# A sliding-window attention and feed-forward kernel: a new order of the first phase, and Q of the last three batches transposed by the DMA crossbar

## The chip, the cores and the metric

The kernel runs on one core of a Trainium2 chip. The metric is the time of one execution in device microseconds (us); lower is better. The profiled execution also has a span, from its first to its last instruction, which is one or two microseconds below the time. PE is TensorE's matmul stream, PEld its weight loads, DVE is VectorE, ACT is ScalarE, POOL is GpSimd and SP is SyncE, which issues most of the DMAs.

## The reference

Eight batches of eight heads, 576 positions, head size 64. Each query sees itself and the 63 positions before it. The result of the attention, 4608 rows of 512, goes through a feed-forward part without a nonlinearity other than a product:

```python
scores = scale * np.matmul(q, k.transpose(0, 1, 3, 2))
rel = pos[:, None] - pos[None, :]
mask = (rel >= 0) & (rel < 64)
attn = softmax(np.where(mask, scores, -1e9))        # cut: written out in the reference
x = (attn @ v).transpose(0, 2, 1, 3).reshape(B * S, H * D)
a = x @ w1
b = x @ w2
h = a * b @ w3
return h @ w_out
```

## The kernel before

The kernel folds `w3 @ w_out` into one matrix `wc` in its first phase. From there it runs as one pipeline. A tick places half a step of attention among the matmuls of the feed-forward part (FFN), twelve ticks to a batch. Q and K come as float32 rows, are cast to float16, transposed by TensorE into PSUM and copied back:

```python
def big_rows(which, b, hh):
    return {"k": k, "q": q, "v": v}[which][b, hh:H:2].rearrange("j (p r) d -> p j (r d)", r=TI)   # p (32) is outermost

def load_qk(b, which, gate=None, other=None):
    t = sb.tile([P, 2, TI * D], FP32, name="stage", bufs=3)
    ...
    for hh in range(2):
        (other if hh and other else nc.sync).dma_start(out=t[:, hh], in_=big_rows(which, b, hh))

def load_v(b, *blocks):                 # GpSimd's queue: casts on the way, rows of 64
    vh = v_heads(b)
    for c in blocks:
        ...
        nc.gpsimd.dma_start(out=vh[lo:P, c], in_=v[b, :, s0:s0 + P - lo, :].rearrange("h s d -> s h d"))

def copy_v(b, c):                       # the overlap of two blocks of V, on VectorE
    vh = v_heads(b)
    dve_cp(vh[0:D, c], vh[D:P, c - 1])
    if c == 1:
        dve_cp(vh[D:P, 1], vh[0:D, 2])

def transposes(b, which, *cs, into=None, cps=None):
    ...
    for c, tp in zip(cs, into):
        for i in range(6):
            nc.tensor.transpose(tp[:, i, :], t16[:, 6 * c + i, :], ident16)
    # cut: the copies out of PSUM
```

The events of a batch stand in a table. The key is the tick; each event names how many batches ahead it works:

```python
late = {0: [("t", 1, "k", 0), ("cast", 1, "q", 0)], 1: [("cast", 1, "q", 1)],
        2: [("t", 1, "k", 1), ("load", 2, "k")], 4: [("t", 1, "k", 2), ("v", 1, 0, 2, 3)],
        5: [("load", 2, "q")], 6: [("t", 1, "q", 0), ("v", 1, 4, 5)], 7: [("cast", 2, "k", 0)],
        8: [("t", 1, "q", 1), ("copy", 1, 4)], 9: [("copy", 1, 1), ("cast", 2, "k", 1)], 10: [("t", 1, "q", 2)]}
```

The output leaves in blocks of 128 rows from three buffers named `t2k`, filled by VectorE and stored from SyncE's queue, the one that also loads K and Q:

```python
def store():
    while stores:
        r0, c0, c1, o_sb = stores.pop(0)
        queue = nc.scalar if c1 - c0 < DM and c0 == 0 else nc.sync
        queue.dma_start(out=out[r0:r0 + P, c0:c1], in_=o_sb[:, c0:c1])
```

## Time and profile before

| | before |
|---|---|
| time, median of 3 runs | 292.44 us (292.0 to 293.64) |
| span of the profiled execution | 291.4 us |
| TensorE busy | 275.1 us, 94% |
| next busiest: VectorE, GpSimd | 183.6 us, 180.0 us |
| V of batch 5, issue to landing | 2.6 to 4.5 us |

### The profile page before, as it was taken

What the parts mean: (1) busy time and instruction counts of PE and PEld (TensorE: products, weight loads), DVE (VectorE), ACT (ScalarE), POOL (GpSimd) and SP (SyncE); (2) the same over time, 40 slices, a digit from 0 to 9 for tenths busy, and PEclk for the clock granted to TensorE, in tenths of its full rate; (3) what the DMA queues carried; (4) which work ended last, traced back from release to release, by engine and by line L of the source; (5) the groups of instructions that cost most, each with busy time, mean ns of one, the idle gap of its engine ahead of it and who ended that gap; (6) DMA issues with size and microseconds to landing.
All of it is one profiled execution on the core that took longest, in us unless ns stands there. A gap on an engine that the chain in (4) does not pass through costs nothing.

```text
span 291.4 us, 6248 instructions
## 1 busy us (share of the span) xinstructions
PE 275.1 (94%) x2429; PEld 161.4 (55%) x2429; DVE 183.6 (63%) x280; ACT 167.9 (58%) x277; POOL 180.0 (62%) x215
## 2 busy tenths in 40 slices
PE   7589998989899999999999999999999999999992
PEld 7468885445554555555555787455555545444441
DVE  0946558635868477678687856587866655454531
ACT  2565644675267746866777556487567765642300
POOL 8779933599479938695789363786596444402200
PEclk9999999999999999999999999999999999999998
DMA  6999999919697848194849560940094011002013
GB/s 242 247 209 204 207 217 374 168 14 94 152 364 126 77 131 317 12 107 131 311 30 126 168 231 0 187 44 2 37 165 30 2 73 73 2 36 110 2 39 112
DMA packets 48449, 37.68 MB, mean 129 GB/s; under 512 B 34160, under 2 KB 38512, under 8 KB 48416
## 3 DMA queue, kind: packets, MB, share of 16 engines
q0 software_dynamic: 38960, 11.14, 37.1%
q1 hardware_dynamic: 9024, 24.79, 23.4%
q10 hardware_dynamic: 432, 1.31, 1.3%
q8 instruction: 20, 0.33, 0.4%
q14 instruction: 13, 0.11, 0.1%
HBM read 38.80 MB, written 9.44 MB: 166 GB/s over the span
## 4 chain that ended last, share of the span: by engine, by line
PE 80%; POOL 7%; DVE 6%; ACT 2%; DMA 2%; issue 1%; DVEq 0%; POOLq 0%; SPq 0%; ACTq 0%
PE f_ps L432 38%; PE f_ps L450 20%; PE o_ps L354 5%; PE tp L262 5%; PE f_ps L501 5%; PE s_ps L296 4%; POOL pt L310 2%; POOL pt L308 2%; DMA stage<-in_k_dram 2%; DVE kT L266 1%; POOL v L241 1%; DVE k L229 1%; ACT pt L300 1%; PE f_ps L492 1%; PE s_ps L338 1%
## 5 line engine op out<-in xcount | busy, mean ns | idle before, releaser
L432 PE MATMUL f_ps<-xT,w_sb 128*128 128x512 f16 (+1 forms) x640 | 134.4, 358 | 0.0
L308 POOL TENSOR_SCALAR_AFFINE_SELECT pt<-pt 128x512 f16<-128x512 f16 (+1 forms) x64 | 52.5, 820 | 62.3 <-ACT pt L300 62.3
L432 PEld LDWEIGHTS <-w_sb 128*128 128x128 f16 x640 | 59.7, 98 | 50.3 <-issue 0.3
L450 PE MATMUL f_ps<-wc_sb,ab 128*128 128x512 f16 (+1 forms) x296 | 67.0, 373 | 0.1
L438 DVE TENSOR_TENSOR ab<-f_ps,a_sb 128x512 f16<-128x512 f32 x72 | 49.8, 691 | 22.1 <-PE f_ps L432 18.6
L300 ACT ACTIVATE pt<-s_ps 128x1024 f16<-128x1024 f32 (+1 forms) x48 | 45.7, 952 | 21.5 <-PE s_ps L296 19.1
L437 ACT COPY a_sb<-f_ps 128x512 f32<-128x512 f32 x72 | 41.7, 580 | 27.8 <-PE f_ps L432 26.8
L310 POOL TENSOR_SCALAR_AFFINE_SELECT pt<-pt 128x512 f16<-128x512 f16 (+1 forms) x64 | 52.1, 814 | 4.5
L363 DVE TENSOR_TENSOR xT<-o_ps,r 64x384 f16<-64x384 f32 x36 | 19.8, 550 | 39.8 <-ACT r L362 39.8
L450 PEld LDWEIGHTS <-ab 128*128 128x128 f16 x296 | 27.5, 98 | 27.9 <-issue 0.3
L360 ACT ACTIVATE ln_s<-o_ps 64x384 f32<-64x384 f32 x36 | 17.5, 487 | 32.6 <-PE o_ps L354 32.6
L452 DVE COPY t2k<-f_ps 128x512 f32<-128x512 f32 (+1 forms) x36 | 24.5, 682 | 11.8 <-PE f_ps L450 11.4
L241 POOL DMA_DIRECT2D v<-in_v_dram x35 | 29.6, 861 | 0.0
L354 PEld LDWEIGHTS <-v 128*128 128x128 f16 x288 | 18.1, 98 | 8.7 <-ACT pt L300 0.8
L296 PEld LDWEIGHTS <-kT 64*128 64x128 f16 x384 | 10.9, 94 | 18.6 <-issue 16.8
L354 PE MATMUL o_ps<-pt,v 128*128 128x128 f16 (+1 forms) x288 | 20.7, 215 | 0.4 <-DVE xT L364 0.4
L226 POOL CAST k<-stage 128x1152 f16<-128x1152 f32 x12 | 13.7, 1150 | 11.0 <-PE s_ps L262 8.1
L364 DVE TENSOR_TENSOR xT<-o_ps,r 64x384 f16<-64x384 f32 x36 | 20.2, 561 | 0.5
L296 PE MATMUL s_ps<-qT,kT 64*128 64x128 f16 (+1 forms) x384 | 18.2, 214 | 1.8 <-ACT pt L300 1.4
L362 ACT ACTIVATE r<-ln_s 128x384 f32<-128x384 f32 x36 | 18.8, 523 | 1.1
L361 ACT ACTIVATE ln_s<-o_ps 64x384 f32<-64x384 f32 x36 | 17.4, 482 | 0.4
L266 DVE COPY kT<-tp 128x768 f16<-128x768 f16 x18 | 17.1, 950 | 0.0
(88 smaller groups left out, 236.5 us busy)
## 6 DMA issues: line engine op xcount, KB each, us to landing
out_dram<-t2k SPq DMA_DIRECT2D x35, 256.0 KB
stage<-in_k_dram SPq DMA_DIRECT2D x13, 576.0 KB
stage<-in_q_dram SPq DMA_DIRECT2D x13, 576.0 KB
v<-in_v_dram POOLq DMA_DIRECT2D x28, 128.0 KB, 4.3
w_sb<-in_moe_w_dram POOLq DMA_DIRECT2D x4, 512.0 KB, 11.1
ab<-in_moe_w_dram POOLq DMA_DIRECT2D x2, 512.0 KB, 10.7
ab<-in_moe_w_out_dram POOLq DMA_DIRECT2D x2, 512.0 KB, 14.5
xT<-in_moe_w_dram POOLq DMA_DIRECT2D x2, 512.0 KB, 16.3
```

Source lines behind the costliest of these rows:

```text
L241: nc.gpsimd.dma_start(out=vh[lo:P, c], in_=v[b, :, s0:s0 + P - lo, :].rearrange("h s d -> s h d"))
L296: nc.tensor.matmul(s_ps[:, a, jj, c0:c0 + n], kT[half, j, k0:k0 + P], qT[half, j, q0:q0 + n], start=True, stop=True, skip_group_check=True)
L300: nc.scalar.activation(pt[:, :, :, 0:w], s_ps[:, :, :, 0:w], AF.Exp, bias=-SHIFT, scale=scale)
L308: nc.gpsimd.affine_select(out=sl, in_=sl, pattern=pat, compare_op=ALU.is_ge, fill=0.0, base=off, channel_multiplier=-1)
L310: nc.gpsimd.affine_select(out=sl, in_=sl, pattern=[[-s, m] for s, m in pat], compare_op=ALU.is_ge, fill=0.0, base=63 - off, channel_multip ...
L354: nc.tensor.matmul(o_ps[:, jj, o0:o0 + n], v16[:, si * 2 + bi, j0 + jj, a * D:a * D + P], pt[:, a, jj, c0:c0 + n], start=first, stop=(bi = ...
L364: nc.vector.tensor_tensor(xs[D:P], o_ps[D:P, :, 192:384], r[D:P], ALU.mult)
L432: nc.tensor.matmul(d[:, f * n + c0:f * n + c1], w[:, dc, (fc + f) * P:(fc + f + 1) * P], xT[:, dc, xc:xc + c1 - c0], start=first, stop=(dc ...
L437: act_cp(a_sb[:, 0:nf * n], a_ps[:, 0:nf * n])
L438: nc.vector.tensor_tensor(ab[:, fc:fc + nf, lo:hi], b_ps[:, 0:nf * n].rearrange("p (f n) -> p f n", f=nf), a_sb[:, 0:nf * n].rearrange("p ...
L450: nc.tensor.matmul(o_ps[:, 0:c1 - c0], ab[:, fc, t * P:t * P + P], wc_sb[:, fc, c0:c1], start=(fc == 0), stop=(fc == 7))
L452: cp(o_sb[:, c0:c1], o_ps[:, 0:c1 - c0])
```

## The change

Part one reorders the first phase: casts and copies a little earlier, an FFN unit between each two steps that depend on each other, and the second buffer of V filled with ones earlier. Part two lets the DMA crossbar transpose Q of batches 5 to 7 (`CROSSED = 5`), so that TensorE and the copies out of PSUM are spared that work. One such transpose is called a crossing below. Positions 0 to 511 of each batch are crossed in one go; positions 512 to 575 are loaded together (`"last"`) and crossed together, and that for all eight batches. To let the crossbar write plain rows, the queries stay in a permuted order in the scores, and the exponential puts them back in order.

```diff
+    def crossed(b, which):
+        return which == "q" and (b == "last" or b >= CROSSED)
     ...
         for hh in range(2):
-            (other if hh and other else nc.sync).dma_start(out=t[:, hh], in_=big_rows(which, b, hh))
+            if not crossed(b, which):
+                (other if hh and other else nc.sync).dma_start(out=t[:, hh], in_=big_rows(which, b, hh))
+            elif b == "last":
+                src = q.rearrange("b (j e) s d -> e (b j) s d", e=2)[hh, :, TP * QI:S]
+                nc.sync.dma_start(out=t[:, hh, 0:QI * D], in_=src.rearrange("j (p r) d -> j p (r d)", r=QI))
+            else:
+                nc.sync.dma_start(out=t[:, hh, 0:QI * D],
+                                  in_=q[b, hh:H:2, 0:TP * QI].rearrange("j (p r) d -> j p (r d)", r=QI))
     ...
+    def turn(b):
+        t = ...                                             # cut: a tile of the pool "rows" or "vT"
+        tr = t.rearrange("p a n -> p (a n)")[:, 0:QI * P].rearrange("p (i n) -> p i n", i=QI)
+        nc.sync.dma_start_transpose(tr, t16s["q", b][:, 0:QI].rearrange("q i n -> q (i n)"))
+        turned["q", b] = tr
     ...
+                    nc.tensor.matmul(o[:, :, 0:mid - p0], kT[half, j, k0:k0 + P], qT[half, :, TP * j + p0:TP * j + mid], ...)
+                    if p1 > TP:                             # the queries past 512 lie in the other tile
+                        nc.tensor.matmul(o[:, :, mid - p0:p1 - p0], kT[half, j, k0:k0 + P], turned["q", "last"][...], ...)
     ...
-    late = {0: [("t", 1, "k", 0), ("cast", 1, "q", 0)], 1: [("cast", 1, "q", 1)],
-            2: [("t", 1, "k", 1), ("load", 2, "k")], 4: [("t", 1, "k", 2), ("v", 1, 0, 2, 3)],
+    late = {0: [("t", 1, "k", 0), ("cast", 1, "q", 0)],
+            1: [("cast", 1, "q", 1), ("turn", 1), ("load", "last", "q")],
+            2: [("t", 1, "k", 1), ("load", 2, "k")],
+            3: [("cast", "last", "q", 0, pool_cp), ("cast", "last", "q", 1, pool_cp), ("turn", "last")],
+            4: [("t", 1, "k", 2), ("v", 1, 0, 2, 3)],
     ... (the first phase; its part that matters below:)
     scores(6)
-    ffn_ab(0, 3)
-    scores(7)
     copy_v(1, 1)
     ...
+    ffn_ab(0, 3)
+    scores(7)
+    copy_v(1, 4)
     ffn_ab(0, 4)
     scores(8)
-    copy_v(1, 4)
```

## The prediction

> **What bounds the kernel now.** I read the stretches first: the busy time of each engine in nine windows of the span (columns: stretch, its length, then busy microseconds and instruction counts of PE, PEld, DVE, ACT and POOL, the granted clock, the DMA share, GB/s).
>
> ```profile
> 0.00:20.00 20.00, 14.30 (x195) 12.87 (x195) 9.26 (x9) 9.46 (x11) 15.89 (x23) 1.00 0.99 235
> 20.00:44.10 24.10, 22.89 (x327) 19.60 (x325) 14.51 (x24) 13.06 (x23) 18.77 (x24) 1.00 1.23 212
> 44.10:78.80 34.70, 31.24 (x314) 17.05 (x313) 21.70 (x32) 18.51 (x30) 23.39 (x27) 1.00 0.91 158
> ...
> 120.00:160.00 40.00, 40.00 (x336) 21.34 (x335) 30.35 (x46) 28.22 (x48) 33.49 (x38) 1.00 0.74 129
> 160.00:200.00 40.00, 40.00 (x367) 26.83 (x365) 28.45 (x45) 25.24 (x43) 23.73 (x29) 1.00 0.52 116
> 200.00:240.00 40.00, 40.00 (x319) 20.49 (x317) 26.99 (x44) 27.96 (x48) 25.53 (x33) 1.00 0.35 56
> ```
>
> From 120 to 240 us TensorE has no gap and no other engine is full. There every microsecond taken from TensorE is a microsecond of the end, and one taken from another engine is nothing. Gaps lie in the first 79 us: 5.7, 1.2 and 3.5 us in the first three stretches. I then read TensorE's timeline there for what ends each gap (columns: start, length, instruction, count, idle time before it and its releaser):
>
> ```profile
> 22.46 0.51 PE L262 MATMUL o_ps<-ident,k 128*128 128x128 f16 x6 [1.02 <-DVE k L226]
> ...
> 49.94 0.50 PE L262 MATMUL o_ps<-ident,q 128*128 128x128 f16 x6 [1.19 <-DVE q L226]
> 50.27 0.50 PE L262 MATMUL tp<-ident,q 128*128 128x128 f16 x6
> 50.61 0.50 PE L262 MATMUL s_ps<-ident,q 128*128 128x128 f16 x6
> ...
> 61.07 0.40 PE L296 MATMUL s_ps<-qT,kT 64*128 64x128 f16 x8 [1.06 <-ACT pt L300]
> ...
> 78.16 0.49 PE L262 MATMUL tp<-ident,q 128*128 128x128 f16 x6 [0.98 <-DVE kT L266]
> ```
>
> All four are matters of order: a cast or copy on VectorE placed too late (22.5 and 49.9), scores too close behind the previous ones for their only PSUM buffer (61.1), one transposition bank still being emptied (78.2). Third, the DMA of 39 to 59 us, in 40 slices of half a microsecond:
>
> ```profile
> DMA  9999999999999999999999999999999999980000
> GB/s 209 207 203 205 207 238 194 173 325 326 409 345 387 360 372 390 370 379 373 398 369 382 353 398 362 390 369 328 198 158 153 154 147 77 50 53 0 0 0 0
> ```
>
> SyncE's loads of K and Q (576 KB each) run at 330 to 400 GB/s until about 53 us; what follows to 57 us is V of batch 1. Its blocks, issued from 34.8 us, took 19.5 to 20.2 us to land (54.3 for the first, about 55.5 for the second); V of batch 2 took 2.6 to 4.6.
>
> [...]
> [...]above, six transpositions start every 0.34 us, 56 ns each.
> [...]
> [...]
> [...]
>
> **Part one, the order of the first phase.** Engine by engine, in the new program order with the old durations:
> - The memset of the second V buffer (2.7 us) moves ahead of GpSimd's weight loads. The first K and Q loads keep the DMA engines full to about 9 us (396 to 433 GB/s from 3.5 to 8.5), so a weight load issued at 6.7 instead of 4.0 finds its turn at about the same time. I count nothing.
> - Weight folding of blocks 2 and 3 now stands before V's transpositions, where four dummy matmuls (0.2) and the wait of 1.02 were. VectorE reaches the cast of V later, so part comes back: I estimate the phase's last fold ends near 42.4, not 44.1.
> - K and Q of batch 1 are cast before they are needed: the 1.19 us gap goes. Scores 6 then run at about 49.7 instead of 52.8, 3 us early.
> - Here a new wait takes it back. The copies between V blocks of batch 1 now follow scores 6 directly on VectorE, at about 50.4, and their data lands at about 55.5, because GpSimd's issue and SyncE's traffic do not move. VectorE stands in order behind them: copies 0.3 + 0.4, then the product of FFN block 3, 0.69, done near 56.9. TensorE has three FFN banks; it can finish block 4 and scores 8 (about 54.2), but block 5 needs the bank which that product frees. It starts near 56.9; before it started at 57.3. Of 3 us, 0.4 is left and TensorE idles about 2.7.
> - From there to the first FFN product of the next group TensorE has seven units of 1.73, three scores of 0.33, six values of 0.5 to 0.57 and six transposition groups of 0.34: 12.1 + 1.0 + 3.3 + 2.0 = 18.4 us. Before, this took 57.3 to 78.8, 21.5, the difference being the gaps of 1.06, 0.98 and 0.23 and smaller ones. The new order sets an FFN unit between each dependent pair, so I take 18.5: 75.4 instead of 78.8.
> GpSimd must keep pace: from scores 6 on it has 19.9 us of masking, casts and V issues, as before (54.1 to 74.0); begun near 51.1 it ends near 71, and the last values need it at 71.8. It just fits.
> Part one: **-3.4 us**.
>
> **Part two, Q of batches 5 to 7 through the crossbar.** These groups carry it (count, then busy us and mean ns):
>
> ```profile
> L262 PE MATMUL tp<-ident,q 128*128 128x128 f16 x108 | 9.1, 220 | 1.0 <-DVE kT L266 1.0
> L266 DVE COPY qT<-tp 128x768 f16<-128x768 f16 x11 | 10.4, 948 | 0.1
> L300 ACT ACTIVATE pt<-s_ps 128x768 f16<-128x768 f32 x16 | 13.0, 811 | 5.3 <-PE s_ps L296 4.9
> L226 POOL CAST q<-stage 128x1152 f16<-128x1152 f32 x12 | 13.4, 1147 | 0.1
> ```
>
> - TensorE loses 3 x 18 = 54 transpositions: 54 x 56 ns = 3.0 us, all in the gapless stretch.
> - It gains matmuls: queries past 512 lie in another tile, so in the last third of each batch one 128-column matmul of each head becomes two of 64: 8 heads x 3 batches = 24 more. In the timeline eight score matmuls of 128 columns take 0.33 us (41 ns each); four of 128 and four of 64 take 0.27, so a 64 costs 26 ns. A split costs 2 x 26 - 41 = 11 ns; 24 of them 0.26 us.
> - Strides: the moving operand is read in runs of eight halves (16 bytes)[...]; split outputs are runs of four floats.[...] I count 0, as the least certain term.
> - VectorE loses 6 copies (5.7 us), ScalarE 3 of 0.81. ScalarE's exponential of the first third is split in two (512 columns about 0.58, 256 about 0.37, by its copies of those sizes): 0.95 for 0.81, six times, +0.8. It reads PSUM with a step, but its strided copies of 768 elements take 809 ns, just what a plain 768 exponential takes, so the step is free. None of it is on the path.
> - GpSimd: six casts shorter by a ninth (-0.8), two more (+2.0). The new ones stand among the masks near 148 us, where GpSimd is 84% busy; they wait for their own load and the crossbar's read of the previous tile. Three ticks of 2.4 us lie between scores and values, so about 4 us of delay is absorbed.
> - DMA: four transposes of 512 KB.[...] The first is ready at about 142 (cast before: 139.9 to 142.2) and needed near 166: 23 us of slack.
> Part two: -3.0 + 0.26 = **-2.7 us**.
>
> Sum: -3.4 - 2.7 = -6.1, from 292.4 to 286.3. I add half a microsecond for small waits in a rearranged pipeline: **286.8**.
>
> **The rivals.**
> - V lands earlier, or VectorE is not held: then part one could reach 5.5 us and the end 284. For: 3 us lie ready at scores 6. Against: the DMA stays full to 57, and GpSimd's 19.9 us chain then binds about 2 us later.
> - Strided matmuls are slow. If the 18 score units of three batches took double (0.33 us more), 6 us come back and the time is 292.[...]
> - The crossbar takes over 20 us a transpose, or holds SyncE's queue. GpSimd's cast into the same tile then waits in order ahead of the masks, TensorE stops twice or more: 295 to 310. For: it is untested here, and K of batch 6 queues behind it.[...]
> - The early memset delays the first weights: at most 2.7 us at the start, 289.
>
> **Range and chances.** The two gains are nearly independent. With both halved the time is 289.5; with V early 284; the slow crossbar, one in twelve, lies outside. Range 283.0 to 291.5. The 2% line is 286.6, almost on my centre: faster 0.46, same 0.46, slower 0.08.
>
> **What would show each step.** Right: scores 6 near 50 us, then a TensorE gap of 2 to 3 us ahead of FFN block 5 that traces back to V's landing; the next group's first FFN product near 75.5; TensorE gapless from 120 on; 54 fewer transpositions and 24 more score matmuls; crossbar DMAs landing in single microseconds. Wrong: no such gap; score matmuls of batches 5 to 7 well above 0.33 us for eight; idle on TensorE near 150 to 190 released by GpSimd or a DMA.

Its sum came to -3.4 - 2.7 = -6.1 us, from 292.4 to 286.3, and to 286.8 with half a microsecond added for small waits.

## More of the kernel before

The page cuts the span in 40 slices of about 7.3 us; a digit is the busy share in tenths. Two of its rows are TensorE's busy share and the clock granted to it:

```profile
PE   7589998989899999999999999999999999999992
PEclk9999999999999999999999999999999999999998
```

After the first third no slice but the last is below nine tenths, and the clock falls only in the last. SyncE's timeline in the middle of the kernel (start, length of issue, what it issues, how many) becomes important later:

```profile
135.83 1.27 SPq L210 DMA_DIRECT2D stage<-in_k_dram  x2
...
137.88 1.19 SPq L210 DMA_DIRECT2D stage<-in_q_dram  x2
...
156.33 2.54 SPq L459 DMA_DIRECT2D out_dram<-t2k  x2
```

K and Q of batch 6 are asked for at 136 to 139 us, in a pause between two groups of output stores. Another view, of the instructions that touch V from 140 to 175 us, gives the times of its loads:

```profile
L241 POOL DMA_DIRECT2D v<-in_v_dram x5: 692/896/900, 149.1 to 154.7; - x5
...
DMA to landing us min/median/max: 2.6/3.6/4.5
```

V of batch 5 is issued from 149.1 us on, when the Q load of 137.9 is done, and lands within 4.5 us.

## The result, and the profile after

The changed kernel takes 312.85 us (median of 4 runs, 311.27 to 314.76) against 292.22 us for the kernel before in the same rounds: 7% slower. The ratio is 1.0703, with a 95% interval of 1.0625 to 1.0781. A ratio here and below is the mean time of one kernel's fast runs over that of the other's fast runs of the same rounds, so it is not quite the ratio of the medians quoted. The prediction, 286.8 with a range up to 291.5, was wrong.

The same two rows of the page, now with slices of 7.7 us:

```profile
PE   8699999699999999999870599949999999999994
PEclk9999999999999999999996599987999999999999
```

Slices 21 to 23 hold a hole, slice 27 another. The granted clock falls to 0.6 and 0.5 in slices 22 and 23, and to 0.8 and 0.7 around slice 28. The stretches say how much (columns: stretch, its length, busy us and instruction counts of PE, PEld, DVE, ACT, POOL, granted clock, DMA share, GB/s):

```profile
120.00:160.00 40.00, 38.17 (x306) 19.72 (x307) 25.35 (x39) 26.45 (x44) 31.04 (x37) 1.00 0.89 153
160.00:200.00 40.00, 26.91 (x240) 19.70 (x238) 18.55 (x30) 13.35 (x26) 15.14 (x19) 0.83 0.46 110
200.00:240.00 40.00, 36.13 (x273) 18.36 (x272) 22.20 (x37) 23.65 (x42) 26.34 (x31) 0.91 0.71 99
```

Before, these three read 40.00 each at clock 1.00. The chain of work that ended last, by engine and by line:

```profile
PE 62%; DMA 21%; POOL 8%; ACT 3%; DVE 3%; issue 1%; SPq 1%; DVEq 0%; ACTq 0%; POOLq 0%
PE f_ps L485 33%; PE f_ps L503 16%; DMA v<-in_v_dram 13%; PE o_ps L396 4%; DMA stage<-in_q_dram 4%; DMA out_dram<-t2k 3%; PE tp L283 3%; POOL pt L350 3%; POOL pt L352 3%; PE s_ps L325 2%; PE s_ps L318 2%; POOL w_sb L524 1%; ACT pt L335 1%; POOL v L254 1%; DVE t2k L505 1%
```

Before, PE had 80% of that chain and DMA 2%. Now the load of V alone has 13%, and the stores of the output appear. TensorE's timeline has these gaps (the bracket is the idle time before the instruction and what released it), VectorE's timeline the wait behind the largest of them, and the view of V the reason:

```profile
57.44 1.89 PE L485 MATMUL f_ps<-xT,w_sb 128*128 128x512 f16 x8 [2.99 <-DVE ab L491]
...
151.30 0.61 PE L396 MATMUL o_ps<-pt,v 128*128 128x128 f16 x8 [1.45 <-POOL pt L352]
...
173.76 1.01 PE L396 MATMUL o_ps<-pt,v 128*128 128x128 f16 x8 [13.09 <-DVE xT L406]
...
207.97 3.57 PE L485 MATMUL f_ps<-xT,w_sb 128*128 128x512 f16 x8 [3.87 <-DVE t2k L505]
```

```profile
171.57 0.29 DVE L258 COPY v<-v 64x512 f16<-64x512 f16 x1 [16.21 <-DMA v<-in_v_dram]
```

```profile
L254 POOL DMA_DIRECT2D v<-in_v_dram x5: 690/893/902, 151.2 to 156.8; - x5
...
DMA to landing us min/median/max: 15.6/16.1/18.6
```

V of batch 5 is issued 2 us later than before, and lands after 16 us where it took 3.6. VectorE waits for it in order, and everything behind that copy waits for VectorE. The eight matmuls at 207.97 take 3.57 us where eight such take 1.89 elsewhere: the half clock (0.50 granted from 208 to 210 us). SyncE's timeline shows what else was given to the DMA engines at that time:

```profile
139.44 2.06 SPq L270 DMA_TRANSPOSE rows<-q  x1
141.56 1.63 SPq L219 DMA_DIRECT2D stage<-in_q_dram  x2
143.23 1.63 SPq L216 DMA_DIRECT2D stage<-in_k_dram  x2
149.06 2.61 SPq L270 DMA_TRANSPOSE vT<-q  x1
151.73 1.22 SPq L221 DMA_DIRECT2D stage<-in_q_dram  x2
155.39 17.44 SPq L512 DMA_DIRECT2D out_dram<-t2k  x2
```

Q of batch 6 (line 221) is asked for at 151.73; before it was 137.88. The crossing ahead of it starts at 149.06, when GpSimd's casts of the rows past 512 end (from 146.82, 2.22 us). The Q load now falls on V's issue, and on the output stores. Near the end of V's wait, from 162 to 174 us, the DMA engines' busy share in tenths and their GB/s were:

```profile
DMA  2332232232232232232232234466566541100199
GB/s 71 99 99 84 85 112 84 85 112 84 85 112 84 85 111 84 85 112 84 85 102 83 79 69 62 47 38 39 38 38 38 38 27 10 10 0 0 68 403 369
```

Until 168 us that is two or three tenths of the engines, while V is still outstanding.

The books balance within a microsecond. The gaps over 0.3 us between 130 and 240 us sum to 1.45 + 0.38 + 13.09 + 3.87 = 18.8 us; before there were none there. TensorE's busy time rose from 275.1 to 277.1 although 2.7 us of work were taken away, so I estimate that the slow clock cost about 4.7. Less those 2.7 us and the 2.2 us by which the next group's first FFN product came earlier (76.61, before 78.83), this makes 18.6; the spans differ by 309.5 - 291.4 = 18.1 us.

### The profile page after: what moved, and what is told of

It reads as the page before. It is cut to its first block, busy times and chain, and to the rows that moved or that the text cites. A ratio compares the mean times of both kernels' runs of the same rounds, so it can differ in the third digit from the quotient of the medians.

```text
span 309.5 us, 6191 instructions
## 1 busy us (share of the span) xinstructions
PE 277.1 (90%) x2395; PEld 159.7 (52%) x2395; DVE 170.7 (55%) x270; ACT 168.2 (54%) x284; POOL 180.8 (58%) x217
## 4 chain that ended last, share of the span: by engine, by line
PE 62%; DMA 21%; POOL 8%; ACT 3%; DVE 3%; issue 1%; SPq 1%; DVEq 0%; ACTq 0%; POOLq 0%
PE f_ps L485 33%; PE f_ps L503 16%; DMA v<-in_v_dram 13%; PE o_ps L396 4%; DMA stage<-in_q_dram 4%; DMA out_dram<-t2k 3%; PE tp L283 3%; POOL pt L350 3%; POOL pt L352 3%; PE s_ps L325 2%; PE s_ps L318 2%; POOL w_sb L524 1%; ACT pt L335 1%; POOL v L254 1%; DVE t2k L505 1%
## 5 line engine op out<-in xcount | busy, mean ns | idle before, releaser
L485 PE MATMUL f_ps<-xT,w_sb 128*128 128x512 f16 (+1 forms) x640 | 138.5, 367 | 6.9 <-DVE t2k L505 3.9
L485 PEld LDWEIGHTS <-w_sb 128*128 128x128 f16 x640 | 61.3, 100 | 59.8 <-issue 9.4
L491 DVE TENSOR_TENSOR ab<-f_ps,a_sb 128x512 f16<-128x512 f32 x72 | 49.7, 692 | 23.1 <-PE f_ps L485 21.2
L402 ACT ACTIVATE ln_s<-o_ps 64x384 f32<-64x384 f32 x36 | 17.5, 487 | 49.7 <-PE o_ps L396 49.7
L335 ACT ACTIVATE pt<-s_ps 128x1024 f16<-128x1024 f32 (+1 forms) x30 | 28.5, 952 | 14.1 <-PE s_ps L318 13.3
L396 PE MATMUL o_ps<-pt,v 128*128 128x128 f16 (+1 forms) x288 | 21.5, 220 | 15.3 <-DVE xT L406 13.5
L341 ACT ACTIVATE pt<-s_ps 128x1024 f16<-128x1024 f32 (+2 forms) x24 | 17.5, 756 | 9.2 <-PE s_ps L325 6.6
L406 DVE TENSOR_TENSOR xT<-o_ps,r 64x384 f16<-64x384 f32 x36 | 20.2, 560 | 0.5
L239 POOL CAST k<-stage 128x1152 f16<-128x1152 f32 x12 | 13.7, 1148 | 10.5 <-DMA stage<-in_k_dram 7.4
L404 ACT ACTIVATE r<-ln_s 128x384 f32<-128x384 f32 x36 | 18.8, 522 | 1.1
L258 DVE COPY v<-v 64x512 f16<-64x512 f16 x14 | 7.0, 499 | 21.6 <-DMA v<-in_v_dram 21.2
L287 DVE COPY kT<-tp 128x768 f16<-128x768 f16 x19 | 18.1, 951 | 0.0
L239 POOL CAST q<-stage 128x1024 f16<-128x1024 f32 (+1 forms) x14 | 14.8, 1084 | 4.9 <-DMA stage<-in_q_dram 4.8
```

The costliest lines, as they stand in the source:

```text
L239: cp(t16_of(b, which)[:, 0:n, hh * D:hh * D + D], raws[which, b][:, hh, 0:n * D].rearrange("p (i d) -> p i d", d=D))
L335: nc.scalar.activation(pt[:, :, :, 0:w], s_ps[:, :, :, 0:w], AF.Exp, bias=-SHIFT, scale=scale)
L396: nc.tensor.matmul(o_ps[:, jj, o0:o0 + n], v16[:, si * 2 + bi, j0 + jj, a * D:a * D + P], pt[:, a, jj, c0:c0 + n], start=first, stop=(bi = ...
L406: nc.vector.tensor_tensor(xs[D:P], o_ps[D:P, :, 192:384], r[D:P], ALU.mult)
L485: nc.tensor.matmul(d[:, f * n + c0:f * n + c1], w[:, dc, (fc + f) * P:(fc + f + 1) * P], xT[:, dc, xc:xc + c1 - c0], start=first, stop=(dc ...
L491: nc.vector.tensor_tensor(ab[:, fc:fc + nf, lo:hi], b_ps[:, 0:nf * n].rearrange("p (f n) -> p f n", f=nf), a_sb[:, 0:nf * n].rearrange("p ...
```

## The experiments

The first theory (N in the expectations) had one cause: the new Q load is slow, and V waits behind it. What the trace showed for it was the stretch from 162 to 168 us above, where two or three tenths of the DMA engines' time and 71 to 112 GB/s were used while V was outstanding. The new load has the four head pairs `j` outermost, the old one had 32 row groups. Below, the first is called a narrow load, the second a wide one. That this difference makes the load slow was my assumption at that point, and I had not priced it when I predicted; wide_q and narrow_only test it. The rivals: the crossings hold the DMA engines or SyncE (X), the extra Q load and its casts hold GpSimd's masks (L), strided matmuls (S), or the first phase. That the early crossings delay SyncE's loads became a theory of its own (Q) only after wide_q.

**wide_q.** The changed kernel, each Q load split by head pair, so that 32 rows are outermost:

```diff
-                nc.sync.dma_start(out=t[:, hh, 0:QI * D],
-                                  in_=q[b, hh:H:2, 0:TP * QI].rearrange("j (p r) d -> j p (r d)", r=QI))
+                for j in range(NJ):
+                    nc.sync.dma_start(out=t[TP * j:TP * j + TP, hh, 0:QI * D],
+                                      in_=q[b, 2 * j + hh, 0:TP * QI].rearrange("(p r) d -> p (r d)", r=QI))
```

> The changed kernel with one thing undone: Q of batches 5 to 7 is loaded by one DMA for each of the four head pairs (outermost dimension 32 rows) and no longer by one DMA whose outermost dimension is the 4 head pairs. Bytes, layout, crossbar transposes and all else stay. Theory N[...]: V lands in 3 to 6 us instead of 16 to 19, the TensorE gaps of 13.1 and 3.9 us and the half-clock stretch go, time 286 to 289. Rival X (the crossbar transposes hold the DMA engines or SyncE): nothing changes, 308 to 314. Rival L (the extra Q load and its casts on GpSimd hold the masks): the gap of 1.45 and half of the rest stay, 300 to 308.

Measured: 300.58 us (298.43 to 301.77), ratio 1.0255 [1.0183, 1.0328]. 12 us come back, and the expectation is still missed by 12; the number lies in the range of rival L. On TensorE's timeline the gap by GpSimd's masks stays, as L said (1.66 us at 152.22), but the largest gap, though smaller, is still at the same place in the program, behind V:

```profile
166.13 1.01 PE L397 MATMUL o_ps<-pt,v 128*128 128x128 f16 x8 [4.53 <-DVE xT L407]
```

V took 6.1 to 9.6 us. The load of Q of batch 6 stood at 152.44, as late as in the changed kernel. So width is a large part, not all.

**narrow_only.** The kernel before, with only Q of batches 5 to 7 loaded as the change loads it (all 576 rows, transposed by TensorE as ever; the copies out of PSUM take the other column order, cut here):

```diff
+            if which == "q" and b >= 5:
+                nc.sync.dma_start(out=t[:, hh], in_=q[b, hh:H:2].rearrange("j (p r) d -> j p (r d)", r=TI))
+            else:
                 (other if hh and other else nc.sync).dma_start(out=t[:, hh], in_=big_rows(which, b, hh))
```

> The kernel before with one thing added: Q of batches 5 to 7 is loaded with the 4 head pairs as the outermost dimension, as in the changed kernel but with all 576 rows; TensorE still transposes, and the copies behind it take the other column order. No crossbar, no extra load, old order. Theory N: V of batches 5 to 7 lands in 10 to 19 us, TensorE waits 10 us or more, time 300 to 312. Rivals X and L: 291.5 to 293.5, no change.

Measured: 296.29 us (294.14 to 298.55), ratio 1.0104 [1.0018, 1.019]. The direction is right, the size far below the expectation: 4 us by the medians (within 2%), not 8 to 20. In the profiled run 1.5 us of it were lost before any narrow load, at a lower clock near the start (0.7 in the page's second and third slices; the transposition that began at 49.94 us before began at 51.49), so the narrow loads themselves cost nearer 3. The stretch from 148 to 154 us, some 6 us after the load was issued (141.68 in this run):

```profile
148.00:154.00 6.00, 6.00 (x57) 3.24 (x54) 4.75 (x8) 4.84 (x8) 4.49 (x5) 1.00 0.37 110
```

The kernel before moved its K and Q at 369 GB/s from 138 to 144 us and was done. Here the load goes on at 110 GB/s with 0.37 of the engines busy. From 148 to 151 us, before V's issue, SyncE's queue alone took 25.2% of the engines' time and moved 101 GB/s. V, issued from 151.7 us, took 6.5 to 9.5 us (median 9.2). A narrow load at the old place does harm, but modest harm.

**order_only.** Part one alone, by `CROSSED = 8` (no batch is crossed).

```diff
-    CROSSED = 5
+    CROSSED = 8
```

> The changed kernel without any crossbar (the limit from which batches are crossed set past the last): only the new order of the first phase. The changed kernel's trace has the first product of the second FFN group at 76.6 us against 78.8 before, so 2.2 us earlier. Theory N says that this lead holds to the end: 289.5 to 290.8. If the new order hurts later (another rival): 292 or more.

Measured: 292.46 us (290.87 to 293.09), ratio 0.9967 [0.9911, 1.0024]: 1 us or nothing, where I expected at least 1.7. The predicted gap ahead of FFN block 5 was there, 3.35 us at 57.73, and TensorE ran at half clock after it: the mean clock from 58 to 70 us was 0.78 in the profiled run. The fastest of the four runs (290.87) had a clock of 0.998, the other three 0.982 to 0.988.

**cross_only_wide.** Part two alone, with wide loads, on the old first phase (the edit is the change without the first phase's reordering, plus the edit of wide_q).

> The old order of the first phase, Q of batches 5 to 7 through the crossbar, with the wide loads. Theory N and the prediction's sum: 54 transpositions less, 24 short matmuls more, minus 2.7 us: 289.2 to 290.5. Rival X: 300 or more. Rival S (strided operands slow the matmuls): 291 to 296, with score matmuls of the crossed batches well above 0.33 us for eight.

Measured: 301.17 us (299.45 to 303.17), ratio 1.0287 [1.0212, 1.0363]. The expectation fell, and rival X's range (300 or more) holds the number: even with wide loads and the old first phase, the crossing as it is placed costs 8.6 us. The largest gap is 4.68 us at 167.26. That is the time of wide_q (300.58), so the first phase has no part in the loss.

**later_turn_wide.** The test of theory Q: wide_q with the crossing moved behind the Q load of tick 5, and the rows past 512 loaded, cast and crossed later:

```diff
-            1: [("cast", 1, "q", 1), ("turn", 1), ("load", "last", "q")],
+            1: [("cast", 1, "q", 1)],
-            3: [("cast", "last", "q", 0, pool_cp), ("cast", "last", "q", 1, pool_cp), ("turn", "last")],
-            5: [("load", 2, "q")], 6: [("t", 1, "q", 0), ("v", 1, 4, 5)], ...
+            5: [("load", 2, "q")], 6: [("t", 1, "q", 0), ("turn", 1), ("load", "last", "q"), ("v", 1, 4, 5)], ...
+            10: [("t", 1, "q", 2), ("cast", "last", "q", 0, pool_cp), ("cast", "last", "q", 1, pool_cp), ("turn", "last")]}
```

> wide_q with only the place of the crossbar work in SyncE's queue changed: each turn now stands behind the Q load of its tick instead of in front of it, and the extra load, its casts and its turn come half a batch later. Theory Q (in wide_q the turn waits in SyncE's queue for GpSimd's cast, so that the Q load of the next batch slips from 138 us to 152 us, onto V's loads at 152 to 157; together with the extra load that GpSimd waits 4.7 us for): Q load of batch 6 back before 142 us, V of batch 5 lands in under 5.5 us, no TensorE gap over 0.5 us after 90 us, time 287 to 290. Rival X (the crossbar transposes themselves cost the time, wherever they stand): 297 to 302, as wide_q. Rival S (strided operands): no gaps, but 292 or more.

Measured: 291.97 us (291.73 to 292.7), ratio 0.9954 [0.9911, 0.9997]. Q of batch 6 is asked for at 138.18 again, V of batch 5 lands in 2.9 to 5.8 us, and the holes near 170 are gone:

```profile
138.18 5.85 SPq L222 DMA_DIRECT2D stage<-in_q_dram  x8
```

```profile
DMA to landing us min/median/max: 2.9/5.2/5.8
```

So the crossings do not cost the time wherever they stand (rival X as put here: 297 to 302). Rival S (292 or more, without gaps) is answered further down by the length of a score unit. The time misses its range because of the gap at 57.96 (3.35 us) and of two gaps (0.52 and 1.53) near 222, where the crossing of batch 7 at 209.66 met V of batch 7.

**later_turn.** The same order with the narrow loads of the change.

> The same with the changed kernel's own narrow Q loads (4 head pairs outermost). Tells how the two causes add. narrow_only lost 1% to the narrow loads alone, in the old order. Theory N + Q: the narrow load now starts early, so it costs what it cost there, 3 to 5 us over later_turn_wide: 291 to 295. If the order was the only cause: as later_turn_wide. If the narrow load was the larger part: 300 or more.

Measured: 293.16 us (292.63 to 296.88), ratio 1.0025 [0.996, 1.0089], inside its range. But I had expected narrow loads to cost 3 to 5 us over later_turn_wide; it is 1.2 by the medians, and the two intervals overlap. A gap of 2.50 us remains at 161.45, where V of batch 5 takes 8.7 to 10.5 us. With the crossings out of the way of SyncE's loads, a narrow load costs about 1 us more than a wide one. So the two causes don't add: narrow loads cost 12 us in the order of the change and 1 us in this one.

**later_turn_wide_copy.** later_turn_wide with the two copies of V of batch 1 behind scores 8:

```diff
     scores(6)
-    copy_v(1, 1)
     ...
     scores(7)
-    copy_v(1, 4)
     ffn_ab(0, 4)
     scores(8)
+    copy_v(1, 1)
+    copy_v(1, 4)
```

> later_turn_wide with the copies between V blocks of batch 1 moved behind FFN block 4 on VectorE (they stood behind scores 6 and 7). Theory of the prediction's first part (VectorE waits in order for V's landing at about 55 us and TensorE stops 3 us for the bank[...]): the gap of 3.0 to 3.4 us near 57 us goes; GpSimd's chain then binds, so 1 to 3 us less than later_turn_wide: 285 to 288. Rival: GpSimd's chain of masks takes all of it, no change.

Measured: 288.52 us (288.05 to 289.67, 6 runs), ratio 0.9842 [0.9809, 0.9876]. The gap near 57 is gone. Two gaps by GpSimd's masks remain (0.47 and 1.01 us at 65 and 69), and 0.84 at 219.43. The gain over later_turn_wide is 3.45 us by the medians, more than the 1 to 3 expected, and the time is half a microsecond above its range.

**later_turn_wide_copy3.** The same with `CROSSED = 3`, two batches more.

> The same with Q of batches 3 to 7 crossed instead of 5 to 7. 36 transpositions fewer (2.0 us), 16 short matmuls more (0.2): 1.8 us less than later_turn_wide_copy if the stretch is still bound by TensorE alone. Rival (DMA is fuller in batches 2 to 4, or the extra load collides with V there): no gain or a loss.

Measured: 289.8 us (289.29 to 290.73), ratio 0.9875 [0.9841, 0.9909]: no gain but a loss of about 1 us. New gaps stand at 86 to 87 (0.80 and 0.64), 107.9 (0.67) and 218.95 (2.03). The last stands behind V of batch 7, which landed in 6.2 to 9.0 us while VectorE waited 3.9. The first two are GpSimd's masks, which the next run has too with three batches crossed; they were not followed further. So the saving on TensorE is lost again, in part to V landing later.

**early_last_turn.** later_turn_wide_copy, but the crossing of batch 7 stays at tick 1, since no Q load follows it.

```diff
-            turn(b + ahead)
+            if (b + ahead == B - 1) == a[0]:         # a[0]: True in the event of tick 1, False in that of tick 6
+                turn(b + ahead)
```

> later_turn_wide_copy once more, but the crossing of the last batch (7) stays where it was, before the loads of the turn, as no load of Q follows it there. Theory (a crossing holds back whatever load is issued beside it, here V of batch 7): the gap near 220 us (0.84 us in later_turn_wide_copy, 2.05 us in later_turn_wide) goes, V of batch 7 lands in under 5.5 us, and the time is 286.5 to 288. Rival (the gap near 220 has another cause, or the crossing only moves onto another load): the same as later_turn_wide_copy, 288.5.

Measured: 288.08 us (286.52 to 289.84, 6 runs), ratio 0.9828 [0.9776, 0.9879]. The gap near 220 is gone and V of batch 7 lands in 3.5 to 5.6 us (6.0 to 7.3 in later_turn_wide_copy), as the theory said. The stretch that had the largest hole:

```profile
160.00:200.00 40.00, 40.00 (x367) 25.98 (x365) 27.14 (x42) 25.80 (x49) 27.14 (x33) 1.00 0.74 138
```

It is full at clock 1.00, and so is the next, 200 to 240. The time missed its range by a hair, and against later_turn_wide_copy the gain (0.4 us in the medians) is within the spread. This is the fastest version found; it is 1.7% faster than the kernel before, which the interval does not set apart from 2%.

**no_cross_copy.** The control: order_only with the two copies moved, nothing crossed.

> The control for what the crossbar part is worth once its loads no longer collide: the new order of the first phase and the two moved copies of V, but no batch crossed, so all of Q transposed by TensorE as before. Theory: order_only less the gap of 3.35 us near 57.7 and the slow clock after it, 288.5 to 290.5, so that crossing three batches is worth 1 to 3 us against early_last_turn. Rival (the crossing is worth nothing, and all of the gain is the moved copies): equal to early_last_turn within 0.5 us.

Measured: 289.77 us (289.32 to 290.46, 6 runs), ratio 0.988 [0.9835, 0.9925]. So of the gain, 2.7 us come from the first phase with its copies moved, and 1.7 us (by the medians; the intervals of the two ratios overlap, but five of early_last_turn's six runs are below all six of this control, in the same rounds) from crossing three batches. From their common mask gap near 69 us to the end the profiled runs differ by 218.4 - 216.7 = 1.7 us, and early_last_turn lost 1.0 us more to mask gaps near 86 us (0.71 + 0.64 against 0.38): an estimate of 2.6 to 2.7 us for the crossing alone, if those gaps have nothing to do with it; the prediction had 2.7.

By now the theory read: the delayed Q load makes V late, and V makes everything late. The next run was to confirm it from another side.

**v_first.** The changed kernel as it is, with V's loads moved two to three ticks forward, ahead of the casts that GpSimd waits for:

```diff
-            2: [("t", 1, "k", 1), ("load", 2, "k")],
-            3: [("cast", "last", "q", 0, pool_cp), ...
-            4: [("t", 1, "k", 2), ("v", 1, 0, 2, 3)],
+            2: [("v", 1, 0, 2, 3), ("t", 1, "k", 1), ("load", 2, "k")],
+            3: [("v", 1, 4, 5), ("cast", "last", "q", 0, pool_cp), ...
+            4: [("t", 1, "k", 2)],
     # cut: tick 6 loses ("v", 1, 4, 5)
```

> The changed kernel, narrow loads of Q and early crossings kept, with one thing moved: the loads of V of the next batch are issued two to three score steps earlier (at the third and fourth step of a batch, not the fifth and seventh), ahead of the casts of Q that GpSimd waits for, so some 9 us sooner. Theory (the 20 us are V landing late behind the delayed loads of Q): the gap of 13.09 us goes, V may still take 8 to 14 us to land but has the time, and the run takes 293 to 299. Rival (the crossings themselves, or the wait of 4.75 us of GpSimd for the load ahead of its cast, stop the pipeline whatever V does): 305 or more, with a gap of over 5 us left between 145 and 180 us.

Measured: 312.13 us (311.35 to 314.94), ratio 1.0656 [1.0597, 1.0716]. The theory fell: V of batch 5 took 9.8 to 11.3 us, VectorE no longer waited for it, and the kernel was as slow as ever. The number is the rival's, its cause is not. TensorE's timeline, and VectorE's and SyncE's beside it:

```profile
176.56 3.57 PE L485 MATMUL f_ps<-xT,w_sb 128*128 128x256 f16 x16 [9.32 <-DVE t2k L505]
```

```profile
175.82 0.69 DVE L505 COPY t2k<-f_ps 128x512 f32<-128x512 f32 x1 [10.57 <-DMA out_dram<-t2k]
```

```profile
160.11 1.22 SPq L221 DMA_DIRECT2D stage<-in_q_dram  x2
...
162.08 0.83 SPq L512 DMA_DIRECT2D out_dram<-t2k  x2
```

The gap is now released by the copy of an output block, which waited 10.57 us for an earlier store from the same three buffers; the granted clock was 0.50 from 174 to 180 us. That store was issued at 162.08, right behind the narrow Q load in SyncE's queue. The delayed load has a second victim; in the changed kernel it stood in the shadow of the first.

**v_first_wide_copy.** v_first with the wide loads and the moved copies.

> The same earlier loads of V with Q loaded by one DMA for each pair of heads[...] and the two copies of V in the first phase moved behind scores 8: another way to the order of early_last_turn, with the crossings left where the changed kernel has them. Theory: nothing on the path is late any more, 287 to 290, as early_last_turn (288.1). Rival: the wait of GpSimd for the load of the last rows holds its masks, a gap of 1 to 2 us near 150 us remains, 290 to 293.

Measured: 296.2 us (294.27 to 301.75; the last of the four runs, 301.75 us at a clock of 0.976, is slow; the others had 0.992 to 0.999), ratio of the three fast ones 1.006 [1.0004, 1.0117]. Neither range holds it, the rival is nearer: GpSimd's masks, behind its wait for the rows past 512, leave a gap of 2.28 us at 154.78, and 2.13 us at 92. But the gap of 9.32 has shrunk to pieces of 0.35 to 0.67: with wide loads the stores come through sooner, though the second of the two issued from 164.72 us on still ends 4.12 us after the first began.

**v_first_act_store** and **act_store.** v_first, and the changed kernel, with the stores on ScalarE's queue:

```diff
-            queue = nc.scalar if c1 - c0 < DM and c0 == 0 else nc.sync
+            queue = nc.scalar if c1 - c0 == DM or c0 == 0 else nc.sync
```

> v_first with the stores of the output issued from ScalarE's queue, not SyncE's; narrow loads of Q and early crossings stay. Theory (two victims: V, and the stores that stand behind the narrow load of Q in SyncE's queue): the gaps of 9.32 and 4.93 us released by the copy of an output block go[...], and the time is 295 to 301. Rival ([...]a store waits for it from any queue): the gaps stay above 5 us together, 304 or more.

> The changed kernel with only the stores of the output moved to ScalarE's queue; V is loaded where it was. Theory (V is a victim by itself): V of batch 5 still lands after 12 us or more, TensorE's gap near 174 (13.09 us, released by xT behind the copy of V) stays at 8 us or more, the gap of 3.87 near 208 goes, 303 to 310. Rival (V was late only because the stores and the load shared SyncE's queue in that way): V lands in under 8 us and the time is 300 or less.

Measured: 311.52 us (310.15 to 312.78, ratio 1.0619 [1.0552, 1.0685]) and 318.14 us (315.95 to 320.36, ratio 1.0877 [1.081, 1.0945]). Both miss, and both were unclean. Without the first group's stores ahead of it on SyncE, a Q load that stood behind those stores and started at 77 us in the changed kernel started at 49 us, met V of batch 1 and cost a gap of 6.41 (5.25) us near 61. Inside, both did what the theory said: in the first the gap of 9.32 us became 0.58 (2.58 and 4.39 remain one batch later), in the second the gap on V's path stayed at 12.33 and that of the stores shrank to 0.55. I repeated both with that mended.

**v_first_late_store** and **late_store.** Only the stores from the fourth group of rows on go to ScalarE's queue:

```diff
+            queue = nc.scalar if (r0 >= 3 * GT and c1 - c0 == DM) or (c1 - c0 < DM and c0 == 0) else nc.sync
```

> v_first with the output's stores of the fourth group of rows and later on ScalarE's queue; narrow loads of Q and early crossings stay. Theory (the stores stand behind the narrow load in SyncE's queue): the start is as in v_first, with its gap of about 2.7 us near 58; the gap of 9.32 us near 176 is under 1.5 us and no cold clock follows it, which is 12 to 14 us; the second one near 209 (4.93) may be taken by V of batch 6, which in v_first_act_store waited 7.1 us. So 298 to 304. Rival (the gap was moved by the other timing of v_first_act_store, not by the queue): 309 or more.

> The changed kernel with only those stores on ScalarE's queue. Theory (V is by itself a victim, and the stores only wait in its shadow): the gap near 174, released behind the copy of V, stays at 8 us or more; the gap of 3.87 near 208 shrinks or is taken by V of batch 6; 308 to 314. Rival (V was late because of the stores): the gap near 174 under 5 us, 303 or less.

Measured: v_first_late_store 305.51 us (304.54 to 306.3), ratio 1.0444 [1.0383, 1.0504]; late_store 312.29 us (310.67 to 314.37), ratio 1.068 [1.0595, 1.0765]. In the first, TensorE's timeline reads:

```profile
169.31 2.03 PE L485 MATMUL f_ps<-xT,w_sb 128*128 128x256 f16 x16 [0.86 <-DVE t2k L505]
...
206.80 3.57 PE L485 MATMUL f_ps<-xT,w_sb 128*128 128x512 f16 x8 [5.45 <-DVE ab L491]
```

The gap of the stores is 0.86 us where it was 9.32. What is left is one batch later: V of batch 6, whose issue ran beside the narrow Q load of 183.2 us, took 22.6 us (median) to land and made VectorE wait 7.1 us. So the time is 1.5 us above my range. In late_store, with the stores out of the way and V where it was, the gap on V's path is 14.22 us and the time that of the changed kernel, as expected. Each victim is enough by itself to hold the pipeline, and helping one only uncovers the other.

## Why the prediction was wrong

**Part one, the order of the first phase: the mechanism was right, the size was off.** Scores 6 started at 49.84 (predicted 49.7). The new wait behind V of batch 1 was there on VectorE, and made TensorE idle 2.99 us ahead of a start at 57.44 (predicted 2.7 and 56.9):

```profile
54.81 0.87 DVE L258 COPY v<-v 64x512 f16<-64x512 f16 x1 [4.11 <-DMA v<-in_v_dram]
```

The next group's first product started at 76.61 (predicted 75.4), so 2.2 us were won in the trace, not 3.4. Half a microsecond is the later start; the rest is the sum of units, 18.4 us, for work that kept TensorE busy for 19.07. By itself the part measured 1 us or nothing. The term that I had not priced is what such a gap can do to the clock afterwards. Here the length of the gap alone did not decide. After 2.99 us the changed kernel ran on at clock 1.00 (60 to 77 us), after 3.35 us the profiled order_only ran at 0.78 (58 to 70 us). later_turn kept its clock after 3.35 us, and v_first_late_store lost half of it after 2.07 (the same eight matmuls, 1.89 against 3.54 us):

```profile
57.80 1.89 PE L485 MATMUL f_ps<-xT,w_sb 128*128 128x512 f16 x8 [3.35 <-DVE ab L491]
```

```profile
57.48 3.54 PE L485 MATMUL f_ps<-xT,w_sb 128*128 128x512 f16 x8 [2.07 <-DVE ab L491]
```

What decides it was not tested. With the two copies moved the part is worth 2.7 us by the medians (no_cross_copy).

**Part two, the work saved on TensorE: right.** The split and strided score matmuls cost what plain ones do. In the timeline of the changed kernel, the first half of a unit with splits:

```profile
203.69 0.26 PE L325 MATMUL s_ps<-rows,kT 64*128 64x128 f16 x4
203.79 0.19 PE L329 MATMUL s_ps<-vT,kT 64*128 64x64 f16 x2
203.82 0.25 PE L325 MATMUL s_ps<-rows,kT 64*128 64x128 f16 x4
```

The second half starts at 203.82, so four matmuls of 128 columns and two of 64 take 0.13 us, and the whole unit of twelve about 0.3 us, as before. Strides add nothing that the trace shows, as counted. With the collisions removed, crossing three batches is worth 1.7 us by the medians and 2.6 to 2.7 by the estimate above.

**Part two, the DMA: this is the step that failed.** It read "four transposes of 512 KB ... 23 us of slack" and, for GpSimd, "about 4 us of delay is absorbed". Three things were missing.

- It priced the crossings but not the new Q loads beside them, as if only their size had changed. They were slow: 101 GB/s in 25.2% of the engines' time in narrow_only, where the K and Q loads of the kernel before moved 369 in 0.96. In the stretch of 162 to 174 us of the changed kernel the DMA engines were busy 0.36 and moved 85 GB/s, and V landed only from about 170 us on.
- It asked when the crossed Q is needed. What stands behind the crossing in SyncE's queue it named only in a rival ("K of batch 6 queues behind it"). SyncE waits in order for GpSimd's cast (the crossing at 149.06 starts when the casts end), and the rows past 512 put a load, two casts and a crossing more ahead of the Q load of batch 6. The sums had the casts and the crossing, but not the 1 MB of this load. All this moved the Q load of batch 6 from 137.88 to 151.73. GpSimd's wait for the load of the rows past 512, 4.75 us, was absorbed only in part (1.45 and 0.38 us of gaps).
- It took V and the output's stores as given. V took 16 us to land instead of 3.6, and VectorE waited 7.1 us in the changed kernel, 10.57 in v_first, for a store to give its buffer back. That V lands late beside large loads (19.5 to 20.2 us, where V of batch 2 took 2.6 to 4.6) was in the prediction, for batch 1; I did not carry it to the later batches, whose Q load I had moved onto V.

**What the runs showed in its place.** Neither cause alone makes the 20 us. Narrow loads in the old order cost 3 to 4 us (narrow_only); the early crossings with wide loads cost 8.6 (cross_only_wide); both with the new first phase cost 20. Take either away and most returns: width alone 12 us, the later crossings alone 20 (later_turn). It is a meeting in time of a load that is slow with transfers that the pipeline waits for: V in one queue, stores in another. After the gaps of 13.09 and 3.87 us the clock is lower, by the estimate above some 4.7 us more.

**The rivals.** The one that came true was given one chance in twelve: "The crossbar takes over 20 us a transpose, or holds SyncE's queue". Its second half held, the first did not, for in the changed kernel the transfer of a crossing takes about 2.5 us. Even so its range ended at 310. What the prediction held against it was the speed of the crossing, where the order in the queue decided. The rival of strided matmuls did not come true (a unit of 0.3 us), and nothing in these traces pointed to the early memset, which no run tested alone.

**What stays open.** How much of the remaining 12 us of v_first_late_store is V of batch 6 and how much the masks (gaps of 2.46 and 2.29 us) was not taken apart. Nor was it tried whether the crossings alone, placed beside V, would slow it as much as a Q load; the 2 us near 220 in later_turn_wide, gone with the crossing moved in early_last_turn, speak for some of it. later_turn moved the crossings and the load, casts and crossing of the rows past 512 together, so SyncE's order and GpSimd's wait of 4.75 us were not taken apart. v_first_wide_copy, where that wait stays, was 8 us slower than early_last_turn.

## What to carry to other kernels

When a change adds a DMA or reshapes one, price three things: how fast its access pattern runs (here 101 GB/s with the four head pairs outermost in narrow_only, 369 with 32 row groups in the kernel before), what stands behind it in the same in-order queue, and which transfers of other queues will be in flight beside it. Moving a load by 14 us can matter more than its size, so compare the issue times of all loads before and after, not only those of the new instructions. And when a repair leaves the time as it was, read the largest gap again: its releaser may have changed, as it did from V to the stores.

## What this case measured of the hardware

- The first crossing (512 KB) kept the DMA engines full for about 2.5 us, which is some 210 GB/s, where loads of K and Q reach 369. The DMA view of the changed kernel from 140.5 to 143.2 us (the first row is the busy share in 40 slices):

```profile
DMA  0001699999999999999999999999999999999999
...
DMA packets 2002, 0.51 MB, mean 189 GB/s; under 512 B 2002, under 2 KB 2002, under 8 KB 2002
```

  The mean counts the empty start. All packets are under 512 bytes: 0.51 MB over 2002 is 256 bytes each.
- A load that took a quarter of the engines' time (25.2% at 101 GB/s in narrow_only) held V, which landed in 9.2 us there and in 16 us in the changed kernel, not 3.6, and in v_first VectorE waited 10.57 us for a store behind it.
- With the stores on another queue the gap they caused fell from 9.32 to 0.86 us.
- The clock fell to about half after gaps of 2.07 us (v_first_late_store), 2.66 (v_first) and 3.35 (order_only), and stayed at 1.00 after 2.99 (the changed kernel); after 3.35 in later_turn eight matmuls kept their 1.89 us. The length of the gap does not separate the two.
- Split writes in runs of four floats cost nothing measurable, 0.3 us for a unit as before. The reads in runs of 16 bytes and fewer cost nothing either.
